# Sliding-window attention and a gated product on one core: the first batch's q and k loaded in blocks, and wide tiles in the second half of the first product

## The chip, the core and the metric

The kernel runs on one core of a Trainium2 chip. A core has five engines with queues of their own: TensorE (PE) for matmuls and transposes, VectorE (DVE), ScalarE (ACT), GpSimd (POOL) and SyncE (SP). ACT, POOL and SP also issue DMAs. The metric is the device time of one execution in microseconds (us); a lower one is better.

## The reference

```python
# q, k, v: (8, 8, 576, 64) float32: batch, head, position, head dimension
scores = matmul(q, k.T) / sqrt(64)
scores = where((rel >= 0) & (rel < 128), scores + slope[head] * -abs(rel), -1e9)   # rel = query - key
attn   = softmax(scores)
x      = matmul(attn, v)                       # -> (4608 tokens, 512)
h      = x @ w_in                              # w_in (512, 2048)
out    = (h * cos(h)) @ w_out                  # w_out (2048, 512); out (4608, 512) float32
```

Each query sees itself and the 127 positions before it, so a block of 128 queries needs its own block of keys and the one before.

## The kernel before

**Work.** All matmuls are bfloat16. The attention is cut into units: for each batch one unit for query block 0 (all heads), two for each of the blocks 1 to 3 (four heads each), and one for the last 64 queries. A unit is: scores on TensorE (L568), in the first units behind a matmul that adds the bias (L582); the exponential on ACT (L595); where there was no bias matmul, a multiplication by the exponential of bias and mask on DVE (L614); the product with v (L630 to L644); its normalisation on DVE (L667 to L681); and a transposition into xT, on TensorE (L702, L721) with a copy, or by a DMA. The 4608 tokens are then worked off in nine chunks of 512. For a chunk the first product (L759, or L784 in chunk 0) makes h in tiles of 128 by 512, ACT the cosine, DVE the product gT, and the second product (L812) the output. While a chunk is in the second product, the next units of attention run.

**Chunk 0** begins when nothing is there yet. Seven units of batch 0 give its 512 tokens. `moe1_block` (L784) works in tiles of 128 tokens by four column blocks, so that it can begin with the first 128 tokens; each tile is 16 matmuls with 128 columns. In the later chunks `moe1` (L759) takes all 512 tokens for one column block, four matmuls with 512 columns.

**The loads.** For the first two batches q and k come in rows: a partition holds several consecutive positions of one head, and TensorE transposes them. `PIECES` (L355) says in which pieces. For batch 0: the first 128 positions in float32 by SP (q) and ACT (k) into `qF`, cast to bfloat16 by DVE or ACT (L378) into `qC` and transposed whole (L504, four transposes of 128 by 128); then positions 128 to 255, 256 to 511 and 512 to 575 by GpSimd, which casts in the DMA (L383), and transposed half by half (L509). Batch 1 comes in one piece for each of q and k. Batches 2 to 7 come in blocks of 128 tokens with all heads side by side (`load_nat`, L402, into `nat`) and are transposed by DMA. v is loaded in such blocks as well (L391), into `vp`. w_in comes in five pieces (L423; the names in the diff count pieces of 256 columns) and w_out in four (L430), all by GpSimd.

**The order.** GpSimd's operations run in the order of the program text. On the other engines a planner (`Plan.schedule`) orders them at build time: every operation has a duration for the engine that is held (`occ`) and one until its result is there (`lat`), due times of loads are estimated from one running clock of the DMA, and at each step the operation that can begin first, by priority `pri`, is taken; for some copies it also chooses between ACT and DVE. While TensorE would stand still near the start, it inserts matmuls on zeros. `emit` then gives each engine its queue in that order, with semaphore waits. A queue is worked off strictly in order: an instruction that waits holds all behind it.

GpSimd's order before is: constants; q and k positions 128 to 255; v block 0; q and k 256 to 511; v block 1; w_in piece 0; v blocks 2, 3; w_in pieces 1, 2-3, 4-5; the ends of q and k; w_in 6-7; batch 1's q and k rows; v block 4; the four quarters of w_out; batch 1's v; batch 2's q and k.

## Time and profile before

| | |
|---|---|
| time, median of 3 runs | 310.25 us (309.75 to 310.46) |
| the profiled execution: time, and span of the core | 310.24 us, 308.4 us |
| busy: TensorE, ScalarE, VectorE, GpSimd | 299.5, 200.3, 195.8, 97.0 us |
| chunk 0's second product (L812) begins | 36.63 us after the span's start |
| moved by GpSimd's DMAs in the whole span | 18.10 MB in 100688 packets |
| moved by the DMAs of SP | 20.33 MB in 49344 packets |

In the rows below, a group of instructions is named by line, engine, operation and tiles (out<-in), with its count; PEld is TensorE's loading of weights, beside the matmuls. A start is in us from the beginning of the span. A DMA's time to landing runs from its issue on the engine to its completion. Where a row covers several issues, their starts follow from the row's length divided by the count.

### The profile page before, as it was taken

Reading aid. Unit: us, or ns where it says so; the run is one execution under the profiler, and the core shown is the slowest. Engines: PE = TensorE matmul, PEld = TensorE weight load, DVE = VectorE, ACT = ScalarE, POOL = GpSimd, SP = SyncE. Lnnn points to the kernel's source line nnn. Section 1 sums busy time; section 2 is a strip of 40 time slices with the busy share of each in tenths; the row PEclk is TensorE's granted clock in tenths of the full one; section 3 lists DMA queues with packets and bytes.
Section 4 is the critical chain, followed back from the end, with each engine's and each line's share of the span. In section 5 each row is a group of like instructions: output and inputs, shape, how many; then the busy total and the mean of one; then the engine's idle time right before and its main releaser. Section 6 shows DMA issues by size and latency. Waiting matters only on the chain.

```text
span 308.4 us, 6675 instructions
## 1 busy us (share of the span) xinstructions
PE 299.5 (97%) x2685; PEld 162.1 (53%) x2726; DVE 195.8 (63%) x409; ACT 200.3 (65%) x267; POOL 97.0 (31%) x122
## 2 busy tenths in 40 slices
PE   8889999999999999999999999999999999999996
PEld 6679755445554455445544554455445554444444
DVE  7688777574668566856785568656966588742000
ACT  6887973875478745873688378746964488752211
POOL 8997200455055505550347123900500000000000
PEclk9999999999999999999999999999999999999999
DMA  9999999999499958998699969995991420001112
GB/s 147 179 204 207 206 162 193 132 183 154 122 121 138 172 98 154 133 175 98 157 114 149 167 88 180 150 184 114 143 113 44 113 70 0 0 0 70 68 71 99
DMA packets 150333, 39.09 MB, mean 127 GB/s; under 512 B 138912, under 2 KB 145312, under 8 KB 150304
## 3 DMA queue, kind: packets, MB, share of 16 engines
q0 software_dynamic: 100688, 18.10, 79.5%
q1 hardware_dynamic: 49344, 20.33, 33.3%
q8 instruction: 21, 0.34, 0.5%
q10 hardware_dynamic: 272, 0.26, 0.3%
q14 instruction: 8, 0.07, 0.1%
HBM read 36.70 MB, written 9.44 MB: 150 GB/s over the span
## 4 chain that ended last, share of the span: by engine, by line
PE 90%; DMA 3%; POOL 2%; ACT 2%; issue 1%; DVE 1%; POOLq 0%; ACTq 0%
PE ps L812 38%; PE ps L759 36%; PE ps L568 5%; PE ps L784 4%; DMA w_inb<-in_moe_w_in_dram 3%; ACT p L595 2%; PE ps L642 2%; PE ps L644 2%; PE ps L630 1%; POOL vp L391 1%; PE ps L509 1%; DVE p L614 1%; PE ps L634 1%; POOL qrows L383 0%; PE ps L721 0%
## 5 line engine op out<-in xcount | busy, mean ns | idle before, releaser
L812 PE MATMUL ps<-w_outb,gT 128*128 128x512 bf16 (+2 forms) x566 | 132.1, 373 | 2.5 <-issue 1.3
L759 PE MATMUL ps<-xT,w_inb 128*128 128x512 bf16 x499 | 113.9, 379 | 0.7
L768 DVE TENSOR_TENSOR gT<-ps,cos 128x512 bf16<-128x512 f32 x128 | 85.1, 688 | 19.6 <-ACT cos L764 14.7
L764 ACT ACTIVATE cos<-ps,halfpi 128x512 f32<-128x512 f32 x128 | 84.6, 687 | 18.0 <-PE ps L759 13.9
L812 PEld LDWEIGHTS ps<-w_outb,gT 128*128 128x128 bf16 x592 | 53.4, 98 | 55.7 <-DVE ob L820 0.3
L595 ACT ACTIVATE p<-ps 128x1024 bf16<-128x1024 f32 x64 | 61.5, 1023 | 31.2 <-PE ps L568 31.0
L759 PEld LDWEIGHTS ps<-xT,w_inb 128*128 128x128 bf16 x512 | 49.0, 98 | 56.2 <-ACT p L595 0.6
L391 POOL DMA_DIRECT2D vp<-in_v_dram x40 | 33.7, 870 | 87.6 <-DMA xT<-xnat 67.4
L614 DVE TENSOR_TENSOR p<-p,emask 128x1024 bf16<-128x1024 bf16 x59 | 39.7, 684 | 27.8 <-ACT p L595 27.8
L819 ACT ACTIVATE ob<-ps 128x512 f32<-128x512 f32 (+2 forms) x21 | 12.1, 576 | 41.6 <-PE ps L812 35.2
L402 POOL DMA_DIRECT2D qnat<-in_q_dram x30 | 25.3, 877 | 22.5 <-DMA qt<-qnat 22.5
L402 POOL DMA_DIRECT2D knat<-in_k_dram x30 | 25.4, 884 | 12.3 <-DMA kt<-knat 9.8
L820 DVE COPY ob<-ps 128x512 f32<-128x512 f32 x16 | 11.0, 685 | 15.8 <-PE ps L812 15.7
L681 DVE TENSOR_TENSOR xnat<-ps,rec 128x256 bf16<-128x256 f32 x48 | 19.9, 421 | 1.3
L568 PE MATMUL ps<-qt,kt 64*128 64x128 bf16 (+1 forms) x576 | 19.4, 211 | 0.3 <-DVE qt L525 0.2
L642 PEld LDWEIGHTS ps<-vp,p 128*128 128x128 bf16 x192 | 14.2, 97 | 9.9 <-issue 6.4
L568 PEld LDWEIGHTS ps<-qt,kt 64*128 64x128 bf16 x576 | 14.5, 94 | 8.7 <-issue 3.5
L642 PE MATMUL ps<-vp,p 128*128 128x65 bf16 x192 | 17.4, 193 | 0.7 <-DVE xT L731 0.5
L644 PE MATMUL ps<-vp,p 128*128 128x65 bf16 x192 | 17.5, 193 | 0.0
L784 PE MATMUL ps<-xT,w_inb 128*128 128x128 bf16 x256 | 16.0, 219 | 0.6 <-DMA w_inb<-in_moe_w_in_dram 0.6
L784 PEld LDWEIGHTS ps<-xT,w_inb 128*128 128x128 bf16 x256 | 14.5, 98 | 1.3 <-DMA w_inb<-in_moe_w_in_dram 0.8
L644 PEld LDWEIGHTS ps<-vp,p 128*128 128x128 bf16 x192 | 13.2, 97 | 2.2
(66 smaller groups left out, 160.9 us busy)
## 6 DMA issues: line engine op xcount, KB each, us to landing
out_dram<-ob SPq DMA_DIRECT2D x35, 256.0 KB, 2.2
vp<-in_v_dram POOLq DMA_DIRECT2D x32, 128.0 KB, 7.1
qnat<-in_q_dram POOLq DMA_DIRECT2D x24, 128.0 KB, 6.5
knat<-in_k_dram POOLq DMA_DIRECT2D x24, 128.0 KB, 5.1
w_outb<-in_moe_w_out_dram POOLq DMA_DIRECT2D x4, 512.0 KB, 21.8
w_inb<-in_moe_w_in_dram POOLq DMA_DIRECT2D x3, 512.0 KB, 12.2
qrows<-in_q_dram POOLq DMA_DIRECT2D x1, 576.0 KB, 15.5
krows<-in_k_dram POOLq DMA_DIRECT2D x1, 576.0 KB, 17.5
```

The costliest lines, as they stand in the source:

```text
L391: op("pool", [lambda e, t=t, rows=rows: e.dma_start(vp[b % 2][0:rows, t, :, 0:64], v[b, :, 128 * t:128 * t + rows, :].rearrange("h p d -> ...
L402: fns.append(lambda e, t=t, rows=rows: e.dma_start(nat[which][0:rows, t, :, :], src[b, :, 128 * t:128 * t + rows, :].rearrange("h p d -> p ...
L568: ins = e.matmul(ps[:, banks[x], c0:c0 + n_], keys_ap(b, x, pr, kc), query_ap(b, x, pr, qb, n_), start=not acc, stop=stop)
L595: op("act", lambda e: e.activation(P[i][:, 0:1024], ps[:, banks[0]:banks[0] + 2, :].rearrange("p a b -> p (a b)"), ACTF.Exp, scale=0.125), ...
L614: op("dve", lambda e: e.tensor_tensor(p, p, m, ALU.mult), r=[("P", i), ("EM", 0), ("EM", 1)], w=[("P", i)], occ=600, lat=690, pri=1)
L642: e.matmul(o, P[i][:, c0:c0 + 128], V[:, qb - 1, h, 0:65], start=True, stop=False)
L644: ins = e.matmul(o, P[i][:, c0 + 128:c0 + 256], V[:, qb, h, 0:65], start=False, stop=True)
L759: op("pe", lambda e, kc=kc: e.matmul(ps[:, bank, :], w_in[:, kc, 128 * fc:128 * fc + 128], xT[:, kc, r0:r0 + CH], start=(kc == 0), stop=(k ...
L764: op("act", lambda e: e.activation(cosb[ci][:, :], ps[:, bank, :], ACTF.Sin, bias=halfpi[:, 0:1]), r=["halfpi"], w=[("B", bank), ("cos", c ...
L768: op("dve", lambda e: e.tensor_tensor(gT[gi][:, fc, :], ps[:, bank, :], cosb[ci][:, :], ALU.mult), r=[("cos", ci)], w=[("B", bank)] + [("g ...
L784: ins = e.matmul(ps[:, bank, 128 * i:128 * i + 128], w_in[:, kc, 128 * fc:128 * fc + 128], xT[:, kc, t0:t0 + 128], start=(kc == 0), stop=( ...
L812: op("pe", lambda e, t=t, fc=fc, bank=bank, j0=j0, j1=j1: e.matmul(ps[:, bank, 0:j1 - j0], gT[gi][:, fc, 128 * t:128 * t + 128], w_out[:, ...
```

## The change

Batch 0's q and k now come in blocks of 128 positions throughout, in two forms, and each is transposed by four whole 128 by 128 transposes. Blocks 0 and 1 come in rows in float32 by SP (k's block 0 by ACT), with a cast each (`load_first`). Blocks 2, 3 and the half block 4 come by GpSimd in the form of `load_nat`, with all heads of a position side by side (`load_block`), into the buffer `nat`, whose lower half of the last block is zeroed first. GpSimd's queue has no load of block 1 any more, and its order is written as a string. Three memsets of v's buffers and others are ordered behind the constants of the mask. In chunk 0 the second half of the first product (column blocks 8 to 15) uses `moe1`, with 512 tokens to a matmul, in place of `moe1_block`; batch 1's row transposes come one tile later among them. The seven first units are planned one at a time. Some of the planner's durations change.

```diff
-        PIECES = {0: [(0, 4, [(0, 4)]), (128, 4, [(0, 4)]), (256, 8, [(0, 4), (4, 8)]),
-                      (512, 2, [(0, 2)])],
-                  1: [(0, 18, [(0, 5), (5, 10), (10, 14), (14, 18)])]}
+        ROWS = [(4, [(0, 4)]), (18, [(0, 5), (5, 10), (10, 14), (14, 18)])]
...
+        def load_first(which, src, n):
+            x = qF[which][n]
+            act = which == "k" and n == 0
+            op("act" if act else "sp", [lambda e: e.dma_start(x[:, :, :], row_ap(src, 0, 128 * n, 4))],
+               w=[("qF", which, n)], dma=f"ld{which}{n}", occ=2000 if act else 700,
+               lat=3300 if act else 4000 if n == 0 else 3950, pri=0)
+            i = x[:, :, :].rearrange("p y (j d) -> p y j d", j=4)
+            o = qC[which][n][:, :, :, :].rearrange("p j y d -> p y j d")
+            op(("act", "dve"),
+               {"act": lambda e: e.activation(o, i, ACTF.Copy),
+                "dve": lambda e: e.tensor_copy(o, i)},
+               r=[("qF", which, n)], w=[("rows", which, 0, n)], occ={"act": 460, "dve": 330},
+               lat={"act": 560, "dve": 410}, pri=2)
...
+        def load_block(which, src, t):
+            rows = 128 if t < 4 else 64
+            op("pool", [lambda e: e.dma_start(
+                nat[which][0:rows, t, :, :],
+                src[0, :, 128 * t:128 * t + rows, :].rearrange("h p d -> p h d"))],
+               r=[("nend", which)] if t == 4 else [], w=[("nb", which, t)], dma=f"lb{which}{t}",
+               occ=900, lat=7 * rows)
...
                 op("dve", lambda e, i=i: e.memset(vp[i][:, :, :, 64:65], 1.0), w=[("vinit", i)],
-                   pri=5 * i)
+                   pri=5 * i, after=[last])
...
+        def block_transposes(names, t, banks):
+            def f(e):
+                ins = None
+                for which, bank in zip(names, banks):
+                    for pr in range(NPAIR):
+                        ins = e.transpose(
+                            ps[:, bank, :].bitcast(BF16)[:, 128 * pr:128 * pr + 128],
+                            nat[which][:, t, 2 * pr:2 * pr + 2, :].rearrange("p h d -> p (h d)"),
+                            ident[:, :])
+                return ins
...
-            sizes = ([[2] * 4] + GROUPS + [[], []])[phase + 1]
+            sizes = ([[1] * 7] + GROUPS + [[], []])[phase + 1]
...
-        load_qk("q", q, 0, 0)
-        load_qk("k", k, 0, 0)
+        for n in range(2):
+            load_first("q", q, n)
+            load_first("k", k, n)
         constants()
-        load_qk("q", q, 0, 1)
...
-        load_qk("k", k, 0, 3)
+        for x in "q2 v0 k2 v1 w0-1 q3 k3 v2 w1-2 v3 w2-4 w4-6 q4 k4 w6-8 qr kr v4".split():
...
         biases()
         for n in range(2):
-            qk_transposes(0, "q", n, [0], OB[0:1])
-            qk_transposes(0, "k", n, [0], OB[1:2])
-        qk_transposes(0, "k", 2, [0], OB)
+            for which, bank in zip("qk", OB):
+                row_transposes(0, which, [bank], n)
+        for t in range(2, 4):
+            for which, bank in zip("qk", OB):
+                block_transposes([which], t, [bank])
...
-        qk_transposes(0, "qk", 3, [0], UB)
-        load_w_in(6, 8)
-        load_qk("q", q, 1)
-        load_qk("k", k, 1)
-        load_v(0, [4])
+        block_transposes("qk", 4, UB)
...
                 for i, (t, f4) in enumerate(order):
-                    moe1_block(t, f4, seq[at % 6])
+                    if i >= 8:
+                        moe1(0, i, seq[at % 6])
+                    else:
+                        moe1_block(t, f4, seq[at % 6])
                     at += 1
-                    if i in (9, 12):
-                        qk_transposes(1, "q" if i == 9 else "k", 0, range(2),
-                                      UB + [seq[at % 6], seq[(at + 1) % 6]])
+                    if i in (10, 13):
+                        row_transposes(1, "q" if i == 10 else "k",
+                                       UB + [seq[at % 6], seq[(at + 1) % 6]])
```

166 lines of the change are left out of this document (77 added, 89 removed).

## The prediction

> **What bounds the kernel now.** I read the page's head first, then the busy time by stage, the waits of the first 37 us, the chain that ended last, and last the DMA issues with their landings.
>
> ```profile
> span 308.4 us, 6675 instructions
> PE 299.5 (97%) x2685; PEld 162.1 (53%) x2726; DVE 195.8 (63%) x409; ACT 200.3 (65%) x267; POOL 97.0 (31%) x122
> ...
> 9.10:17.30 8.20, 7.19 (x138) 5.25 (x140) 5.97 (x18) 6.61 (x9) 8.20 (x13) 1.00 1.68 187
> ...
> 36.60:308.40 271.80, 266.44 (x2101) 134.18 (x2138) 167.91 (x336) 171.45 (x227) 67.16 (x80) 1.00 1.12 119
> ```
>
> The columns of the stages are the stretch, its length, then busy time of PE, PEld, DVE, ACT and POOL, the granted clock, the DMA share and GB/s. TensorE is busy for 299.5 of 308.4 us. From 36.6 us on nothing in the diff changes an instruction's size, and TensorE is busy for 266.44 of 271.80 us there. So the change is worth what it moves the moment at which the second product (L812) of the first chunk can run through, at 36.6 us and just behind. The granted clock is 1.00 in these stages, so no term of the clock enters.
>
> Before that the DMA share is above 1 (1.68): a stream of transfers issued by GpSimd runs without a gap. Where TensorE waits for it:
>
> ```profile
> PE ps L784 <- DMA w_inb<-in_moe_w_in_dram: 0.6, 1, 0.6
> ...
> 8.61 8.67 DMA w_inb<-in_moe_w_in_dram
> ...
> 8.61 2.27 POOL L423 DMA_DIRECT2D w_inb<-in_moe_w_in_dram  x3
> ...
> 12.97 0.70 POOL L383 DMA_DIRECT2D qrows<-in_q_dram  x1
> 13.66 0.71 POOL L383 DMA_DIRECT2D krows<-in_k_dram  x1
> ...
> 15.07 3.00 POOL L430 DMA_DIRECT2D w_outb<-in_moe_w_out_dram  x4
> ...
> w_inb<-in_moe_w_in_dram POOLq DMA_DIRECT2D x1, 512.0 KB, 10.4
> ...
> qrows<-in_q_dram POOLq DMA_DIRECT2D x1, 576.0 KB, 15.5
> ...
> krows<-in_k_dram POOLq DMA_DIRECT2D x1, 576.0 KB, 17.5
> ...
> w_outb<-in_moe_w_out_dram POOLq DMA_DIRECT2D x1, 512.0 KB, 24.6
> ```
>
> The first two lines are the wait (total, times, longest) and the chain's piece (start, length); then come GpSimd's issues (start, length), and single issues with the time to landing. The second weight piece (256 columns) ends the only DMA wait of any size, at 8.61 + 8.67 = 17.3 us. The transfer behind it, columns 512 to 1023, is issued at about 9.4 and lands 10.4 later, at 19.8. Batch 1's q rows land at 12.97 + 15.5 = 28.5, its k rows at 13.66 + 17.5 = 31.2, the last quarter of w_out (issued at about 17.3) at 41.9.
>
> ```profile
> 19.89 0.22 PE ps L784 x4
> ...
> 23.46 0.34 PE ps L509 x8
> 23.81 5.02 PE ps L784 x88
> 28.83 1.13 PE ps L509 x36
> ...
> 36.63 3.18 PE ps L812 x14
> ...
> 40.87 0.75 PE ps L812 x3
> ...
> 54.26 5.83 PE ps L759 x27
> ```
>
> These are pieces of the chain. From 19.89 to 36.63, 16.74 us, it runs on TensorE nearly unbroken. The third quarter of w_out is first used at 40.87; the program has seven matmuls of 216 ns (5.83/27) there before the first that needs the last quarter, so that one starts at about 42.4, half a microsecond after its landing. TensorE's work and the stream thus run neck and neck up to 42 us. A gain needs both to be earlier.
>
> **The change part by part.** *The stream.* SP now brings second q and k blocks in float32, so GpSimd's two 128 KB transfers go. Its two of 256 KB become four 128-token blocks of 128 KB, laid out like a block of v; the two ends of 64 KB become half blocks.
>
> ```profile
> 3.50:4.00 0.50, 0.00 (x0) 0.00 (x0) 0.16 (x1) 1.00 1.09 364
> 5.50:6.50 1.00, 0.00 (x0) 0.00 (x0) 0.00 (x0) 1.00 2.14 158
> 7.00:8.50 1.50, 0.41 (x8) 0.28 (x8) 0.00 (x0) 1.00 1.16 171
> ...
> 2.91 0.94 POOL L391 DMA_DIRECT2D vp<-in_v_dram  x1
> ...
> 4.53 0.71 POOL L383 DMA_DIRECT2D krows<-in_k_dram  x1
> ...
> 6.13 0.76 POOL L423 DMA_DIRECT2D w_inb<-in_moe_w_in_dram  x1
> 6.87 1.78 POOL L391 DMA_DIRECT2D vp<-in_v_dram  x2
> ...
> vp<-in_v_dram POOLq DMA_DIRECT2D x1, 128.0 KB, 4.3
> ...
> krows<-in_k_dram POOLq DMA_DIRECT2D x1, 256.0 KB, 6.4
> ...
> w_inb<-in_moe_w_in_dram POOLq DMA_DIRECT2D x1, 256.0 KB, 7.1
> ...
> vp<-in_v_dram POOLq DMA_DIRECT2D x1, 128.0 KB, 7.2
> ```
>
> The first three lines (busy columns of one tile only; the last number is the GB/s of all DMA) are the float32 loads of SP and ACT (364 GB/s), a block of v (158), and the 256 KB row pieces (171). Removed: 256 KB + 512 KB + 128 KB at 171 GB/s, so 1.53 + 3.07 + 0.77 us. Added: 512 KB + 128 KB in blocks at 158, so 3.32 + 0.83, and 512 KB of float32 at 364, so 1.44. The sum is +0.22 us. By landings it looks better: v's first block lands at 7.2 and the second piece of k at 10.9, so the two row pieces took 3.7 instead of 3.07, while v's third block took 0.9 (14.1, behind the first weight piece at 13.2), four of them 3.4 to 3.6 with the rate's 0.83 or this; that gives -0.1 to -0.3. The rates are means over the DMA engines, the landing is that of the last one. I take the middle of +0.2 and -0.3: the stream from the weights on is 0.05 us earlier, which is nothing.
>
> All this hangs on whether SP's 1.44 us are paid by the same stream. The row at 3.5 us has a DMA share of 1.09 before GpSimd's data flow, and none of the later rows here lies below that, so I see no idle room and take the full 1.44. The other bound is none of it, -1.5 us in all. The Trainium skill, DMA: Bandwidth & Descriptors, section "Issuing engines are not separate DMA queues", says that DMAs of all issuing engines run on the same 16 DMA engines and that issuing from several saves only sequencer time; by it the sum is mine, and without it the stream would be 1.4 us shorter. The trace agrees only as far as that share goes; no run so far shows both kinds side by side.
>
> Within the stream v's last full block moves behind the second weight piece. That piece is earlier by such a block, about 0.9, and its 0.6 us wait goes.
>
> *What is late next.* In the changed program's order TensorE meets the transfer of columns 512 to 1023 earlier: after 32 small matmuls of the first product, it takes 12 that need it, and only then the probabilities-times-v group of the seventh unit. In the kernel before, that group and 16 matmuls of another tile came first. So TensorE stands in order at that landing, 19.8 - 0.05, and behind it are queued that group, the last transposes of x and all the rest. At 19.89 the old kernel had done the same 32 matmuls, and the group too. From there I count differences.
>
> ```profile
> 18.01 0.19 PE L642 MATMUL ps<-vp,p 128*128 128x65 bf16 x1
> ...
> 18.26 0.38 PE L784 MATMUL ps<-xT,w_inb 128*128 128x128 bf16 x4
> ```
>
> The group costs 0.25 (18.01 to 18.26): +0.25. Half of the first product goes from 128 matmuls of 57 ns (5.02/88), 7.30 us, to 32 of 216 ns, 6.91: -0.39. The 8 half-width transposes of the ends (0.34) become 8 whole ones, at 57 ns 0.46: +0.12. The sum is -0.02, so L812 starts at 19.8 + 16.72 = 36.5, 0.1 earlier. The float32 blocks' and the third and fourth blocks' transposes lie before 19.8 and are hidden in that wait.
>
> Batch 1's rows: their transposes now follow the third wide tile. Counting forward from 19.8, with 96 small matmuls (5.5), the group, four transposes of x and eight of the ends (0.7) and three wide tiles of 0.86, TensorE gets there at 28.8, as before (28.83), after the landing at 28.5. The k rows come 36 transposes (1.13) and two wide tiles later, at 31.7 against 31.2. No wait. The last quarter of w_out now has six matmuls ahead of it, so it is wanted 0.1 + 0.2 earlier, at 42.1, with a landing at 41.85: no wait, but only 0.25 us of room. Whatever else TensorE gained, it would lose there.
>
> *The casts and the attention chain.* Two more casts, on ACT and DVE:
>
> ```profile
> 5.00 0.47 DVE L378 CAST qcast<-qfirst 128x512 bf16<-128x512 f32 x1
> ...
> 11.24 0.59 ACT L524 ACTIVATE qt<-ps 128x512 bf16<-128x512 bf16 x1
> ...
> 13.48 3.03 ACT L595 ACTIVATE p<-ps 128x1024 bf16<-128x1024 f32 x3 [0.88 <-PE ps L568]
> 16.74 1.02 ACT L595 ACTIVATE p<-ps 128x1024 bf16<-128x1024 f32 x1 [0.23 <-PE ps L568]
> ...
> L614 DVE TENSOR_TENSOR p<-p,emask 128x1024 bf16<-128x1024 bf16 x59 | 39.7, 684 | 27.8 <-ACT p L595 27.8
> ```
>
> Each is half a microsecond, on engines that wait for loads then. The order also puts the transposes of the third q and k blocks ahead of the second unit's scores, and those of the fourth ahead of the fourth unit's. The fourth k block is the last of the same bytes that in the old stream ended with the first weight piece, at 6.13 + 7.1 = 13.2. Add 0.2 to 0.5 for four transposes and their way to ACT and 0.59 for a copy: the fourth exponential starts at about 14.3 instead of 13.48, and the seventh ends at about 18.6 instead of 17.8. Its group is then ready at 19.3 with the mask (684 ns), while TensorE stands at the weights until 19.8 and works on them until 20.4. So the casts and the late blocks cost nothing, covered by about 1.1 us of that wait; past that cover they cost one to one. GpSimd's second issue (v) waits for a memset that now comes behind the mask's constants, near 3.1; that issue was at 2.91 with a landing 4.3 later, so the queue holds work by then; I put it at nothing, at most 0.2.
>
> The sum: 310.24 us for the profiled execution (median 310.25, so no correction) less 0.1 is **310.1 us**. A change below 0.2%, 0.62 us, is about what a measurement of this kernel cannot tell from none.
>
> **The rivals.** *SP's loads fit beside GpSimd's.* If the float32 rows mostly use gaps of the DMA engines, the stream is up to 1.5 earlier, columns 512 to 1023 land at 18.3 to 18.8, and L812 starts 1.0 to 1.3 earlier; w_out's last quarter at 40.4 keeps pace. The time is 309.0. For it: the rate of GpSimd's own float32-to-bf16 pieces (171 written, 342 read) lies under the 364 of the float32 loads; and a shorter slowest engine works the same way (the landings above). Against it: the share never falls.
>
> *The small packets cost more.* The blocks move 128-byte rows where the pieces moved 512 bytes and more.
>
> ```profile
> vp<-in_v_dram POOLq DMA_DIRECT2D x1, 128.0 KB, 8.6
> ```
>
> v's fourth block, issued at about 7.75, landed at 16.35, 2.25 behind the third, which had taken 0.9. If the six new small-packet transfers meet one such step more, every later landing is 1.4 later, L812 starts at 37.9 and the time is 311.5; it decides from the point where the stream is 0.6 late. The Trainium skill, DMA: Bandwidth & Descriptors, section "Specifications", puts line rate at transfers of 512 B or more, and has a read-modify-write below. By that rule this rival is likelier than the forecast; the trace has 158 against 171 GB/s, a loss of 8%, in the sum already.
>
> *The attention chain decides.* If the fourth blocks land past 14.3 (13.2 and the cover), the seventh unit's group is late behind the weights' 12 matmuls. At 15.2 this gives +0.9: 311.0. For it: six transfers of a new shape lie ahead of them. Against it: the same bytes have landed by 13.2 before.
>
> **How the numbers follow.** The forecast, within 0.6 us of none, 0.42. SP's loads hidden, wholly or enough, 0.36: the sum of landings already leans to that side. Small packets 0.16 and the chain 0.06, together 0.22 slower. The range is 309.0 to 311.2: it holds the faster rival's full price, the chain and the smaller half of the packets' price, and leaves out about 0.15. The forecast alone would be 309.6 to 310.7.
>
> **What would show it.** Right: TensorE waits some 0.5 to 1.3 us for w_inb at 19 to 20 us in front of 12 matmuls; q rows land at 28 to 29, w_out's last quarter near 41.9; L812 starts at 36.3 to 36.8. Wrong: those landings off by a microsecond either way, or a wait of TensorE before 19 us for exponentials that L812's start inherits.

## The result and the profile after

The changed kernel takes 311.58 us (median of 14 runs, 310.85 to 312.87), the kernel before 310.11 us on the same chip (14 runs, 309.49 to 311.73): a ratio of 1.0046, 95% interval 1.0030 to 1.0062. A second set gave 311.81 against 310.02, 1.0060 (1.0042 to 1.0078). So the change costs about 1.4 to 1.8 us, where 310.1 had been forecast and 309.0 to 311.2 allowed.

The page after, and its busy time by stage (the columns as before):

```profile
span 309.2 us, 6447 instructions
...
PE 299.6 (97%) x2569; PEld 158.0 (51%) x2612; DVE 195.5 (63%) x409; ACT 202.5 (66%) x271; POOL 97.6 (32%) x122
```

```profile
9.10:17.30 8.20, 7.12 (x125) 5.10 (x125) 4.86 (x16) 7.03 (x10) 8.20 (x13) 1.00 1.87 180
36.60:308.40 271.80, 266.59 (x2102) 134.19 (x2138) 167.08 (x335) 172.22 (x228) 67.16 (x80) 1.00 1.10 119
```

The totals hardly differ: 0.1 us more work on TensorE, 0.8 us more span (some forty records of matmuls are missing in each). Where they part is read from the moments at which a chunk's first product begins on TensorE. From the timeline of before, chunks 1, 4 and 7:

```profile
54.10 0.59 PE L759 MATMUL ps<-xT,w_inb 128*128 128x512 bf16 x2
...
148.79 0.59 PE L759 MATMUL ps<-xT,w_inb 128*128 128x512 bf16 x2
...
247.51 0.81 PE L759 MATMUL ps<-xT,w_inb 128*128 128x512 bf16 x3
```

and from that of after, where the first row is chunk 0's second product:

```profile
36.30 0.81 PE L838 MATMUL ps<-w_outb,gT 128*128 128x512 bf16 x3
...
53.81 1.03 PE L785 MATMUL ps<-xT,w_inb 128*128 128x512 bf16 x4
...
149.03 0.38 PE L785 MATMUL ps<-xT,w_inb 128*128 128x512 bf16 x1
...
248.34 0.38 PE L785 MATMUL ps<-xT,w_inb 128*128 128x512 bf16 x1
```

Such a moment shows a lead only where the same work lies behind it. How many matmuls of chunk 0's second product are through when chunk 1 begins can be read from TensorE's weight loads of that line (the second count; each matmul has one, and all 592 of this line are there in every profile). In before, in after, and in e2, an experiment told below:

```profile
36.00:54.10 18.10, 13.55 (x55) 5.12 (x59) 1.00 1.99 181
```

```profile
36.00:53.81 17.81, 13.31 (x54) 4.91 (x57) 1.00 1.91 177
```

```profile
36.00:53.66 17.66, 13.80 (x57) 5.01 (x57) 1.00 1.90 182
```

The changed order puts two of these matmuls, 0.43 us at 216 ns each, behind the beginning of chunk 1. At chunk 4 the counts are equal (245), and at chunk 7 too (439).

The weight loads also put right where chunk 0's second product begins in before. Its first two loads, in before and in after, are

```profile
36.39 0.13 PEld L812 LDWEIGHTS ps<-w_outb,gT 128*128 128x128 bf16 x2 [0.25 <-issue]
```

```profile
36.27 0.13 PEld L838 LDWEIGHTS ps<-w_outb,gT 128*128 128x128 bf16 x2 [0.20 <-issue]
```

In after the first matmul follows its load by 0.03, at 36.30. In before the first record of a matmul is at 36.63, behind both loads: it is the second matmul, and the first, at about 36.42, has no record.

| point | before | after | lead (-) or loss | with the same work behind it |
|---|---|---|---|---|
| chunk 0's second product | 36.42 | 36.30 | -0.12 | -0.12 |
| chunk 1 | 54.10 | 53.81 | -0.29 | +0.14 |
| chunk 4 | 148.79 | 149.03 | +0.24 | +0.24 |
| chunk 7 | 247.51 | 248.34 | +0.83 | +0.83 |
| end of the span | 308.4 | 309.2 | +0.8 | |
| time of the execution | 310.24 | 312.10 | +1.86 | |

So in this execution the second product began 0.12 us earlier, as the prediction said, and at chunk 1 that lead was gone. 0.69 us were lost between 54 and 248 us, in code that the diff leaves alone, and 1.06 us outside the span (the time less the span: 1.84 before, 2.90 after). A second profile of the changed kernel has 53.69 for chunk 1, also with 57, which is level with before, a span of 308.8, and 3.01 outside.

The other executions tell of a third thing: the changed kernel's span is 308.7 to 311.1 us, and at or over 309.9 in 5 of its 20 runs; before it was so in 1 of 130 (307.6 to 310.1, median 308.2). The time outside the span is 1.83 to 1.93 us in all 130 runs of before; in the changed kernel 1.8 to 3.0.

The waits of TensorE in the first 37 us of after, and the stream's issues and landings:

```profile
PE ps L516 <- DVE kcast L374: 0.6, 2, 0.3
PE ps L539 <- DVE qt L498: 0.5, 1, 0.5
...
PE ps L521 <- DMA qrows<-in_q_dram: 0.2, 1, 0.2
```

```profile
10.70 0.82 POOL L427 DMA_DIRECT2D w_inb<-in_moe_w_in_dram  x1
```

```profile
w_inb<-in_moe_w_in_dram POOLq DMA_DIRECT2D x1, 512.0 KB, 8.6
...
qrows<-in_q_dram POOLq DMA_DIRECT2D x1, 576.0 KB, 14.3
...
krows<-in_k_dram POOLq DMA_DIRECT2D x1, 576.0 KB, 16.4
...
qfirst<-in_q_dram SPq DMA_DIRECT2D x2, 256.0 KB, 4.8
...
kfirst<-in_k_dram SPq DMA_DIRECT2D x1, 256.0 KB, 5.5
```

Columns 512 to 1023 of w_in land at 10.70 + 8.6 = 19.3. The waits for w_inb are gone; instead TensorE waits for k's cast and for a copy of q, at 7 to 11 us.

### The profile page after: what moved, and what is told of

It is laid out like the page before. It is cut to its first block, busy times and chain, and to the rows that moved or that the text cites. A ratio compares the mean times of both kernels' runs of the same rounds, so it can differ in the third digit from the quotient of the medians.

```text
span 309.2 us, 6447 instructions
## 1 busy us (share of the span) xinstructions
PE 299.6 (97%) x2569; PEld 158.0 (51%) x2612; DVE 195.5 (63%) x409; ACT 202.5 (66%) x271; POOL 97.6 (32%) x122
## 4 chain that ended last, share of the span: by engine, by line
PE 80%; DMA 8%; POOL 5%; ACT 3%; DVE 2%; issue 1%; POOLq 0%; ACTq 0%
PE ps L785 35%; PE ps L838 35%; DMA w_outb<-in_moe_w_out_dram 8%; PE ps L594 5%; ACT p L621 3%; PE ps L668 2%; PE ps L670 1%; POOL vp L394 1%; POOL w_inb L427 1%; PE ps L656 1%; DVE p L640 1%; POOL knat L385 1%; POOL w_outb L434 1%; PE ps L660 1%; POOL qnat L385 1%
## 5 line engine op out<-in xcount | busy, mean ns | idle before, releaser
L785 PE MATMUL ps<-xT,w_inb 128*128 128x512 bf16 x529 | 121.2, 379 | 1.3 <-DVE rec L705 0.5
L794 DVE TENSOR_TENSOR gT<-ps,cos 128x512 bf16<-128x512 f32 x136 | 90.7, 688 | 21.5 <-ACT cos L790 16.6
L790 ACT ACTIVATE cos<-ps,halfpi 128x512 f32<-128x512 f32 x136 | 90.2, 687 | 19.6 <-PE ps L785 15.4
L785 PEld LDWEIGHTS ps<-xT,w_inb 128*128 128x128 bf16 x544 | 51.8, 98 | 59.9 <-ACT p L621 0.6
L845 ACT ACTIVATE ob<-ps 128x512 f32<-128x512 f32 (+2 forms) x23 | 13.3, 578 | 43.7 <-PE ps L838 43.6
L846 DVE COPY ob<-ps 128x512 f32<-128x512 f32 x14 | 9.6, 687 | 16.2 <-PE ps L838 16.1
L705 DVE RECIPROCAL rec<-ps 128x4 f32<-128x4 f32 x48 | 8.2, 176 | 6.2 <-PE ps L670 5.7
## 6 DMA issues: line engine op xcount, KB each, us to landing
qrows<-in_q_dram POOLq DMA_DIRECT2D x1, 576.0 KB, 14.3
krows<-in_k_dram POOLq DMA_DIRECT2D x1, 576.0 KB, 16.4
```

The costliest lines, as they stand in the source:

```text
L785: op("pe", lambda e, kc=kc: e.matmul(ps[:, bank, :], w_in[:, kc, 128 * fc:128 * fc + 128], xT[:, kc, r0:r0 + CH], start=(kc == 0), stop=(k ...
L790: op("act", lambda e: e.activation(cosb[ci][:, :], ps[:, bank, :], ACTF.Sin, bias=halfpi[:, 0:1]), r=["halfpi"], w=[("B", bank), ("cos", c ...
L794: op("dve", lambda e: e.tensor_tensor(gT[gi][:, fc, :], ps[:, bank, :], cosb[ci][:, :], ALU.mult), r=[("cos", ci)], w=[("B", bank)] + [("g ...
```

## The experiments

In most of them "later order as before" means that every operation planned behind chunk 0's first product takes its engine and its place from a table of the plan of before, so that the first phase alone differs (the code in the excerpts of this section is shortened):

```diff
+                mark = len(R.all)          # chunk 0, ahead of load_nat("q", q, 2)
...
+        R.pin_late(mark)                   # engines from the table
         R.schedule(filler=...)
+        R.order_late(mark)                 # places from the table
```

All kernels, each against before on the same chip; "outside" is time less span, "long" the runs with a span of 309.9 us or more, the last column the matmuls and transposes of TensorE's program (two more than the weight loads on the page of each run):

| kernel | median us | ratio (95%) | span, median | long | outside, median (range) | matmuls |
|---|---|---|---|---|---|---|
| before | 310.06 | | 308.2 | 1 of 130 | 1.88 (1.83 to 1.93) | 2728 |
| changed | 311.58 | 1.0046 (1.0030 to 1.0062) | 309.25 | 4 of 14 | 2.0 (1.8 to 2.9) | 2614 |
| e12, changed again | 311.81 | 1.0060 (1.0042 to 1.0078) | 309.2 | 1 of 6 | 2.54 (1.8 to 3.0) | 2614 |
| e1 | 311.38 | 1.0047 (1.0026 to 1.0068) | 308.85 | 3 of 8 | 2.29 (1.8 to 3.0) | 2614 |
| e2 | 310.85 | 1.0018 (1.0006 to 1.0030) | 308.7 | 0 of 12 | 2.18 (2.1 to 2.3) | 2728 |
| e3 | 310.30 | 1.0002 (0.9989 to 1.0014) | 308.4 | 0 of 12 | 1.88 (1.8 to 2.5) | 2632 |
| e4 | 311.29 | 1.0037 (1.0021 to 1.0053) | 309.35 | 3 of 12 | 2.02 (1.9 to 2.2) | 2710 |
| e5 | 310.52 | 1.0013 (0.9999 to 1.0027) | 308.5 | 1 of 12 | 1.93 (1.8 to 2.3) | 2619 |
| e6 | 313.90 | 1.0111 (1.0089 to 1.0133) | 311.8 | 5 of 5 | 2.11 (2.1 to 2.2) | 2724 |
| e7 | 310.77 | 1.0016 (0.9999 to 1.0033) | 308.35 | 0 of 12 | 2.18 (1.9 to 3.7) | 2614 |
| e8 | 311.00 | 1.0027 (1.0013 to 1.0042) | 309.0 | 1 of 12 | 2.05 (1.8 to 2.1) | 2636 |
| e9 | 311.82 | 1.0056 (1.0044 to 1.0068) | 309.7 | 2 of 6 | 2.15 (2.1 to 2.2) | 2770 |
| e10 | 311.14 | 1.0041 (1.0026 to 1.0056) | 308.65 | 1 of 6 | 2.30 (2.0 to 3.3) | 2619 |
| e11 | 310.93 | 1.0037 (1.0024 to 1.0049) | 308.9 | 0 of 9 | 2.12 (2.0 to 3.5) | 2614 |
| e13 | 310.72 | 1.0013 (1.0000 to 1.0025) | 308.45 | 1 of 12 | 1.96 (1.8 to 2.8) | 2742 |
| e14 | 310.81 | 1.0014 (1.0002 to 1.0027) | 308.8 | 0 of 11 | 1.90 (1.8 to 2.1) | 2635 |
| e15 | 311.04 | 1.0027 (1.0016 to 1.0037) | 309.2 | 0 of 11 | 1.82 (1.8 to 1.9) | 2636 |
| e16 | 310.83 | 1.0023 (1.0011 to 1.0036) | 308.4 | 0 of 10 | 2.50 (2.0 to 3.0) | 2614 |
| e17 | 310.73 | 1.0015 (1.0007 to 1.0024) | 308.7 | 0 of 11 | 2.02 (1.8 to 2.2) | 2662 |
| e18 | 311.04 | 1.0035 (1.0024 to 1.0046) | 308.9 | 0 of 11 | 2.14 (2.1 to 2.2) | 2710 |

### Which part of the change: e1 to e4

**e1** is the changed front with the later order as before. 

> The changed kernel, except that every operation created behind chunk 0's first product (second products, later attention, later chunks) stands on the engine and in the order that it has in the kernel before; the first phase is the changed one. Theory 'late order' (the first phase is no slower, the loss comes from the order that the planner made of chunks 1 to 6): ratio 0.998 to 1.001, the wait of L785 for DVE's rec near 185 us is gone. Theory 'front' (loads, casts and tiles of the first phase cost the time wherever it shows): 1.003 to 1.006 as for the changed kernel. Theory 'ends' (the time outside the span grew by about 0.5 to 1.0 us): 1.002 to 1.003 with a span as before.

**e2** is the reverse: the first phase of before, and the later order from the table of the changed kernel. 

> The kernel before with the changed kernel's order and engines behind chunk 0's first product; first phase and loads as before. Theory 'late order': 1.002 to 1.004, with a wait of the first product for DVE's rec in chunk 5. Theory 'front': 0.999 to 1.001. Theory 'ends': 1.000, time less span about 1.9.

**e3** is before with the wide tiles alone, later order as before:

```diff
-                    moe1_block(t, f4, seq[at % 6])
+                    if i >= 8:
+                        moe1(0, i, seq[at % 6])
+                    else:
+                        moe1_block(t, f4, seq[at % 6])
```

> The kernel before with the 512-token tiles for column blocks 8 to 15 alone (row transposes of batch 1 one tile later), late order as before. By the count of the prediction 0.39 us less on TensorE, of which the last quarter of w_out gives back all but about 0.4: ratio 0.998 to 1.000 under 'late order' and 'front' (if the loads cost); 1.003 or more if the wide tiles are the cause.

**e4** is the changed kernel without the wide tiles (the diff above reversed), later order as before. 

> The changed kernel with the 128-token tiles kept in the second half of chunk 0's first product, late order as before. Beside e1 it shows the wide tiles' worth in the new front: 0.000 to 0.0013 above e1. Theory 'late order': 0.999 to 1.002. Theory 'front' with the loads as the cause: 1.004 to 1.007.

Measured: e1 311.38, e2 310.85, e3 310.30, e4 311.29. The wide tiles are worth nothing that shows. The front alone loses about as much as the whole change, and brings the spread; the later order alone loses 0.2%. The intervals are too wide to say whether the two add up. Chunks 1 and 7 of e2 begin at

```profile
53.66 1.03 PE L927 MATMUL ps<-xT,w_inb 128*128 128x512 bf16 x4
...
247.77 0.81 PE L927 MATMUL ps<-xT,w_inb 128*128 128x512 bf16 x3
```

against 54.10 and 247.51 in before. With two matmuls fewer behind it (57), chunk 1 of e2 is level with before; up to chunk 7 the changed later order loses 0.26 us, with the front of before. In e1, which has the counts of before, they begin 0.38 and 0.41 late. The front's 0.4 and the later order's 0.3 come to 0.7 in these profiles, where the first profile of the changed kernel has 0.83. That one has a wait of 0.5 us at 185 us which e2 and the second profile of the changed kernel don't have; which other places of the order cost the rest stays open. A few tenths between single profiles are also within the spread of the executions (before: 307.6 to 310.1).

e4's profiled execution is one of the long ones (span 310.4), and shows what the first two profiles don't (columns: stretch, length, PE busy, granted clock, DMA share, GB/s; then the longest wait):

```profile
7.00:8.00 1.00, 0.40 (x8) 1.00 2.26 179
8.00:9.00 1.00, 0.40 (x4) 1.00 2.37 151
9.00:10.00 1.00, 0.56 (x10) 1.00 1.94 176
10.00:11.00 1.00, 0.47 (x13) 0.84 1.70 185
11.00:12.00 1.00, 1.00 (x8) 0.50 2.32 157
...
13.00:14.00 1.00, 1.00 (x9) 0.50 1.86 183
```

```profile
PE ps L685 <- DVE kcast L543: 1.8, 2, 1.0
```

k's second block was cast from 8.46 on instead of 7.96, TensorE was busy for less than half of 7 to 11 us, and then the granted clock stood at 0.50 for three microseconds. The second product began at 38.22; in the changed kernel's first profile it had begun at 36.30.

### SP's loads, their landing, and the clock: e5 to e9, e11

**e5**: the changed front, with the second blocks from GpSimd in bfloat16.

```diff
-        for n in range(2):
-            load_first("q", q, n)
-            load_first("k", k, n)
+        load_first("q", q, 0)
+        load_first("k", k, 0)
         constants()
+        load_first("q", q, 1)    # rows by GpSimd into a bfloat16 buffer, transposed in halves
+        load_first("k", k, 1)
```

> The changed front, later order as before, but the second blocks of q and k come as bfloat16 rows by GpSimd at the head of its queue, so that SP's second float32 loads and their casts are gone; the third and fourth blocks stay whole blocks. Theory SP: the float32 second blocks, landing at 7.1 and 7.9 us in place of 5.7 and 6.4 and then cast, use up the 1.1 us that the attention chain had; without them the time is that of before, 309.9 to 310.4, and the runs scatter by about 1.5 us like those of before. Theory blocks: the whole blocks on GpSimd's queue and their transposes cost it; 311.1 to 311.5, as with the changed front (311.38). Theory clock: TensorE's idle stretches at 7 to 11 us let its clock drop in some runs; the gaps at 7.5 to 10 us should be gone here, and the longest runs with them: 310.0 to 310.5.

**e6**: the reverse, before with SP's second blocks alone.

```diff
-            if b == 0 and n == 0:
+            if b == 0 and n < 2:         # SP, float32, and a cast
...
-        load_qk("q", q, 0, 1)
-        load_qk("k", k, 0, 1)
-        load_v(0, [0])
         load_qk("q", q, 0, 2)
+        load_v(0, [0])
```

> The front of before with one thing new: the second blocks of q and k come by SP in float32 and are cast, and GpSimd's queue begins with the third; the third to fifth blocks stay rows as before, tiles and later order as before. Theory SP: 310.9 to 311.4, with runs scattered over 2 us or more. Theory blocks: 309.9 to 310.4. Theory clock: between, by how long TensorE idles at 7 to 11 us: 310.4 to 311.2 with some long runs whose mean granted clock is under 1.00.

**e7**: the changed front with one number changed in the plan.

```diff
-               lat=3300 if act else 4000 if n == 0 else 3950, pri=0)
+               lat=3300 if act else 4000 if n == 0 else 5500, pri=0)
```

> The changed front, later order as before, and one planned number changed: the second float32 blocks are planned to land 5.5 us after their issue, as the trace shows them, in place of 3.95 us. That puts 5 more zero matmuls between the first scores and the second transposes, and sorts some of the first 20 us otherwise; no wait on a load goes. Theory SP: the data still come late, 311.0 to 311.5. Theory order: the cost came from an order planned for data that weren't there, 309.9 to 310.5. Theory clock: partly mended, 310.3 to 311.0.

**e8**: the changed front with zero matmuls in two of its waits.

```diff
+                if which == "q" and n == 1:          # behind the transposes of q's second block
+                    for _ in range(12): e.matmul(ps[:, 3, 384:512], zeros, zeros)
...
+                if us[0][0] == (0, 0, 0):            # behind the first unit's product with v
+                    for _ in range(10): e.matmul(ps[:, 5, 0:128], zeros, zeros)
```

> The changed front, later order as before, with 12 zero matmuls (0.67 us at 56 ns) behind the transposes of q's second block and 10 (0.56 us) behind the first unit's product with v, where TensorE waited 0.32 and 0.53 us in the trace of the changed kernel and 1.0 us twice in a longer run. Nothing else moves. Theory clock: TensorE no longer idles at 7 to 11 us, the granted clock stays 1.00 in all runs, the runs above 311.5 are gone, and the median falls to 310.3 to 310.8. Theories SP and blocks: no gain; 311.1 to 311.7, since the zero matmuls can outlast the waits by 0.3 us.

**e9** is e6 with 46 such matmuls behind the transposes of q's first block. 

> The kernel of the sixth experiment (the front of before, second blocks by SP in float32 with casts: 313.9 us, TensorE idle for 3.0 us up to 9.86 us, granted clock 0.50 from 9 to 15 us) with 46 zero matmuls (2.6 us at 56 ns) put on TensorE into that wait; the data come no earlier. Theory clock (the idle stretch itself lowers the clock, and that is most of the 3.6 us): granted clock 1.00 from 9 to 15 us, 311.0 to 312.0. Theory late data (the chain of exps starts 3 us late, the clock adds little): 313.3 to 314.0.

**e11** is e5 with the second blocks left in float32 and cast, but issued by GpSimd. 

> The changed front, later order as before, with the second blocks still float32 and still cast, TensorE's order up to the second scores nearly unchanged, but the loads issued by GpSimd at the head of its queue in place of SP. Theory landing (what costs is that SP's second loads land late and by a different amount from run to run): they land near 5.7 and 6.5, 310.2 to 310.8 with a scatter under 1.2 us. Theory casts (the two casts and the order that the planner makes with them cost it): 311.0 to 311.5.

Measured: e5 310.52, e6 313.90, e7 310.77, e8 311.00, e9 311.82, e11 310.93. SP's loads alone make before slower by 1.1%, more than the whole change does and more than any of the three theories gave; without them the changed front comes to within 0.13%. Theory blocks falls. In e6 GpSimd's queue begins with row pieces of 256 KB, and k's second block lands 6.9 us after its issue (5.5 in the changed kernel, 5.2 in its second profile, 6.0 in e4); TensorE's wait, and the clock by stretches in e6 and then in e9:

```profile
PE ps L674 <- DVE kcast L548: 3.0, 1, 3.0
```

```profile
9.00:10.00 1.00, 0.14 (x2) 0.50 2.02 165
10.00:11.00 1.00, 1.00 (x12) 0.50 1.63 191
...
14.00:15.00 1.00, 1.00 (x26) 0.50 1.38 206
```

```profile
9.00:10.00 1.00, 1.00 (x22) 1.00 1.78 178
```

In e9 the data come 0.2 us earlier (k is cast from 9.13 on) and the clock stays at 1.00. e6 lay 3.65 us behind before (310.25 there), e9 lies 1.80 behind (310.02), by nothing but matmuls on zeros: so some 1.85 us, less what the 0.2 is worth, were the clock, and the rest goes with the late data. In the changed front the clock falls in a few of the runs. Of the 11 long runs of changed, e12, e1 and e4, four have a mean granted clock of 0.994 or 0.995, as 3 us at 0.50 make it; the other seven have 0.999 or 1.000 and were not caught in a profile, so their cause is open. The changed kernel itself has one such run in 20 (e12), and before one in 130, its only long one (0.994). With zero matmuls 1 of 12 (e8) and 0 of 11 (e15) are long. For the median the clock is no explanation: e8 left the span at 309.0, and its 311.00 lies between its two cases.

e7 moved the median: 308.35 for the span against 308.85 in e1, no long run, and chunk 1 at

```profile
53.61 0.59 PE L954 MATMUL ps<-xT,w_inb 128*128 128x512 bf16 x2
```

0.87 us ahead of e1 (both with 59 matmuls behind it), although the loads land as in e1: about 0.5 of the front's cost was an order planned for a landing 1.55 us too early. VectorE's queue shows how. In the changed kernel, as in e1, five memsets stand between the cast of k's second block and the copy of q's, for which TensorE waits 0.5 us; e7 has them ahead of the cast, while the engine waits for the load anyway. The copy in the changed kernel and in e7:

```profile
9.23 0.69 DVE L498 COPY qt<-ps 128x512 bf16<-128x512 bf16 x1
```

```profile
8.48 0.68 DVE L667 COPY qt<-ps 128x512 bf16<-128x512 bf16 x1
```

e11 lies between (310.93; a span of 308.9, no long run): its second blocks land at 5.6 and 6.5, no run is long, and something of the casts and their order stays, so neither of its two theories holds alone.

### The changed kernel itself: e10, e12

**e10** is the changed kernel with the edit of e5 and its own later order. 

> The changed kernel as it is, its own later order too, but the second blocks of q and k by GpSimd as bfloat16 rows at the head of its queue. With the later order of before this front gave 310.52. If SP's float32 loads are what the change loses by and its later order costs 0.3 to 0.5: 310.6 to 311.0. If its later order costs nothing with this front: 310.2 to 310.6. If the rest of the change loses too: 311.2 or more.

**e12** is the changed kernel, unedited. 

> The changed kernel once more, for a second profile of it: its runs spread over 310.85 to 312.87, and the one profile shows a front that is level with before. If the spread comes from SP's second loads, this profile differs from the first in the same measure as its span: k's second block casts later than 7.96 us where the span is over 309.2, and the exps 4 to 6 start later than 14.76 by as much. If the front is the same while the span differs, the spread is made later. Median 311.2 to 311.8.

e10 gave 311.14, between its cases: beside e5 the changed later order costs 0.6 by the medians (0.9 by the ratios), 0.15 of it in the span and most of the rest outside. e12's profile differs little from the first (k cast at 7.67 and not 7.96, the fourth exponential at 14.77 and 14.76), yet its span is 0.4 shorter, of which the first lost 0.3 between 182 and 213 us, where it has the wait of 0.5 us: that part of the spread is made later, and the front's part must be read from long runs such as e4's.

### The time outside the span: e13 to e18

The transfers behind the end of the changed kernel's span (309.2), by queue:

```profile
q8 instruction: 1, 0.02, 2.1%
q14 instruction: 1, 0.01, 0.7%
```

Nothing of the kernel is left there but fetches of instructions; the second profile (3.01 outside) has the same two at 311 us. In the window from 309 to 313 us before has no transfer; its last fetch on q8 comes at about 280 us. In the whole profile of before q8 moved 0.34 MB in 21 packets, so about 16 KB each.

**e13**: before, with 14 zero matmuls behind everything.

```diff
+            if e == "pe":
+                for _ in range(14): h.matmul(ps[:, 5, 0:128], zeros, zeros)   # behind the last product
```

> The kernel before with 14 zero matmuls appended behind TensorE's last product (0.8 us at 56 ns, within the 2.4 us that the last copy and the last store take behind it). Nothing else changes, no instruction moves. Theory program length (TensorE's instructions come in fetches of 16 KB, and the program of the changed kernel, 114 matmuls shorter, ends just behind the start of a further one): these 14 carry the program of before over such an edge too; the span stays at 307.7 to 308.7, the time outside it goes from 1.88 in all runs to 2.0 to 3.0 in some, the median to 310.2 to 310.9, and a fetch of instructions shows at 305 to 312 us. Theory no such thing (the time outside belongs to the second loads or to the later order): 1.88 in all runs, 310.0 to 310.2.

**e14**: e7 with 21 zero matmuls in its waits. 

> The changed front planned for a landing 5.5 us after the issue (310.77, span 308.35 at the median but 1.9 to 3.7 us outside it), later order as before, with 21 zero matmuls more: 9 ahead of the first scores (TensorE waited 0.58 us there), 5 ahead of the transposes of k's second block (0.35), 7 ahead of those of q's third (0.29 after 0.15 of other waiting). Theory program length: the last fetch comes before 303 us, the time outside falls to 2.0 in all runs, 310.0 to 310.5, with a span of 308.0 to 308.4. Theory no such thing: 310.6 to 311.0 as without them. If the zero matmuls outlast the waits by 0.3 us: 0.3 more in either case.

**e15**: the changed kernel with the 22 zero matmuls of e8. 

> The changed kernel, its own later order, with the 22 zero matmuls of the eighth experiment (12 behind the transposes of q's second block, 10 behind the first unit's product with v). Theory program length: the time outside the span falls from 1.8 to 3.0 (median 2.0 and 2.5 in two sets of runs) to 2.0 to 2.1 in all runs; span 309.0 to 309.4; 311.0 to 311.4. Theory no such thing: 311.5 to 312.0, outside again up to 3.0. Theory clock: besides, no run with a mean granted clock of 0.995 or a span over 310.5.

**e16**: the changed kernel with the one number of e7, all orders left to the planner. 

> The changed kernel with one planned number changed and all orders left to the planner: the second float32 blocks land 5.5 us after their issue in place of 3.95. Theory order in the front: with the later order of before this took the span from 308.85 to 308.35; here it should do the same, span 308.6 to 308.9 and 311.0 to 311.3. If the planner's later order then comes out like that of before by chance (it costs 0.7 us from 54 to 248 us in the changed kernel): 310.4 to 310.8. Theory that the data alone count: 311.5 to 311.9.

e13 shows it: 310.72, the time outside up to 2.8, 2.3 or more in 5 of 12 runs where no run of 130 of before had over 1.93. The stores at the end of before (303 to 309 us), and in e13 with a fetch among them:

```profile
out_dram<-ob SPq DMA_DIRECT2D x1, 192.0 KB, 1.9
out_dram<-ob SPq DMA_DIRECT2D x1, 64.0 KB, 1.6
```

```profile
q8 instruction: 1, 0.02, 1.0%
...
out_dram<-ob SPq DMA_DIRECT2D x1, 192.0 KB, 2.8
out_dram<-ob SPq DMA_DIRECT2D x1, 64.0 KB, 2.4
```

In that execution (span 309.9) the fetch falls before the last stores, which land later and lengthen the span too. The profiled execution of e7 shows it as well: its last chunk began 0.4 us ahead of before, a q8 fetch falls among the last stores, and its span is 309.6:

```profile
out_dram<-ob SPq DMA_DIRECT2D x1, 64.0 KB, 3.2
```

That lengthening TensorE's program calls forth a q8 fetch says that q8 carries TensorE's instructions. Counted over all kernels: with 2614 to 2619 matmuls 31 of 77 runs have 2.3 us or more outside, with any other length but e13's 2742 it is 1 of 233. (2742 is 2614 and 128: the lengths that are hit lie one fetch apart if a fetch holds 128 matmuls and their weight loads, which no row shows.) e15 closes the other side: the same changed kernel, 22 matmuls longer, has 1.76 to 1.86 outside in all 11 runs and takes 311.04. e14 has 1.85 to 2.13, but its zero matmuls cost 0.45 of the span, and at 310.81 nothing is won on e7. e16 has the span (308.4) and keeps the edge (2.0 to 3.0); at 310.83 it lies just above its second case, and the one number in the plan has halved the loss of the change. What stays open is why some kernels, e2 with the program length of before among them, lie at 2.1 to 2.2 throughout, where before has 1.88.

**e17** and **e18** are e7 with the last four tiles wide (`i >= 12`) and with none. 

> The changed front planned for a landing 5.5 us after the issue, later order as before, and only the last four tiles of chunk 0's first product 512 tokens wide instead of eight, which makes TensorE's program 48 matmuls longer (2662). Theory order and program length: span 308.3 to 308.6, 1.85 to 2.1 outside in all runs, 310.2 to 310.6, level with before. If the front itself costs more than the planned landing: 310.8 to 311.2.

> The same with no wide tile (2710 matmuls on TensorE): the kernel of the fourth experiment (311.29, spans 308.4 to 310.7) with the one planned landing changed. Theory order: span 308.3 to 308.7 and no run over 309.8; 310.2 to 310.7. Theory that the late data count, whatever the order: 311.0 to 311.4 and spans up to 310.7 as there.

e17: 310.73, a ratio of 1.0015, the time outside 1.84 to 2.15 and no run over 308.9 of span: level with e5, still 0.15% behind before. e18: 311.04, not the 310.2 to 310.7 of theory order: its profiled run had a span of 308.1, but three others 309.5 to 309.7. Against e4 the planned landing took the longest spans away (up to 310.7 there) and 0.45 from the median span, of which 0.25 shows in the time. No version beats before.

## Why the prediction was wrong

**The stream: right.** Forecast for the transfer of columns 512 to 1023 was 19.75, measured 19.3; q's rows 28.5, measured 28.7 (14.39 + 14.3); k's rows 31.2, measured 31.4 (14.99 + 16.4). No landing was a microsecond early, so the rival at 309.0 fell. What the shared transfer cost beyond the forecast was paid by SP's loads themselves, which came later. The Trainium skill, DMA: Bandwidth & Descriptors, section "Issuing engines are not separate DMA queues", says that DMAs started by different engines run on the same 16 DMA engines and interleave. The runs agree: the load of k's second block took 4.9 to 6.2 us beside GpSimd's queue of the changed front (e18, e17), 6.9 beside that of e6, and the same bytes at the head of GpSimd's own queue 4.3 (e11).

The sign that was to go with it is missing. TensorE was to wait 0.5 to 1.3 us for w_inb at 19 to 20 us; in after it comes there a tenth of a microsecond before the landing:

```profile
19.07 0.28 PE L747 MATMUL ps<-ident,xnat 128*128 128x128 bf16 x2
19.31 0.84 PE L810 MATMUL ps<-xT,w_inb 128*128 128x128 bf16 x12
```

The wait that was to cover late data had been used up by then.

**The wide tiles, the group, the ends: right.** -0.02 forecast; e3 measured nothing (1.0002).

**The start of the second product: right in the profiled execution, in part by luck.** It was to begin 0.1 earlier and began 0.12 earlier (36.30; the forecast of 36.5 counts from 36.63, 0.21 too late). But the landing came 0.45 sooner than forecast, and the way from there took 17.0 us, where before has 16.5 from 19.89; 0.2 of the difference is a wait for batch 1's q rows, where the working had none. The last quarter of w_out had 0.25 us of room in the forecast, and the small lead ran into it as said; the chain of after has

```profile
18.57 23.65 DMA w_outb<-in_moe_w_out_dram
...
42.27 1.04 PE ps L838 x4
```

a landing at 42.22, 0.37 later than forecast, with TensorE behind it. That is where the lead ended: the twentieth weight load of the second product is 0.13 us ahead of before, the twenty-fourth 0.18 behind.

**"So the casts and the late blocks cost nothing, covered by about 1.1 us": the first step that failed, as a bound.** The second unit's scores in before and in after, the casts, and the exponentials of after:

```profile
8.45 0.40 PE L568 MATMUL ps<-qt,kt 64*128 64x128 bf16 x8 [0.16 <-DVE qt L525]
```

```profile
10.82 0.40 PE L594 MATMUL ps<-qt,kt 64*128 64x128 bf16 x8
```

```profile
7.96 0.54 DVE L374 CAST kcast<-kfirst 128x512 bf16<-128x512 f32 x1 [0.69 <-DMA kfirst<-in_k_dram]
```

```profile
7.17 0.63 ACT L373 ACTIVATE qcast<-qfirst 128x512 bf16<-128x512 f32 x1 [0.75 <-DMA qfirst<-in_q_dram]
...
14.76 2.97 ACT L621 ACTIVATE p<-ps 128x1024 bf16<-128x1024 f32 x3
...
17.89 1.03 ACT L621 ACTIVATE p<-ps 128x1024 bf16<-128x1024 f32 x1
```

The size of a cast was right, the fourth exponential 0.46 late on the forecast of 14.3, the seventh's end 0.3 (18.92 against 18.6), and in this execution the cover held. But the working costed the casts and the fourth blocks, and never asked when SP's second blocks land. They land at about 7.1 and 7.9, where GpSimd's were at 5.7 and 6.4 (issued at 1.36 and 2.2, 4.3 and 4.2 to landing), and TensorE, in order, stands at them: the second unit's scores start at 10.82 in place of 8.45. In e5, without SP's loads, they start at 8.91, so about 1.9 of the 2.4 us belong to those loads and the order around them, on a chain whose cover was 1.1; in this execution what else came earlier made it good. The order planned for the early landing cost about 0.5 of span (e7 against e1). In e4 a landing half a microsecond later went with a fallen clock and a second product 1.9 us later. Late data alone don't do that: in e17, planned for the later landing, k's second block took 6.2 us and TensorE waited 1.0 us for it, yet the clock stayed at 1.00 and the second product began at 36.18.

**"No term of the clock enters": failed in a part of the runs.** It was read off stages in which TensorE was busy. After the idle stretch that the change made at 7 to 11 us the granted clock dropped to 0.50 for 3 us in e4, and for 6 in e6; e9 puts a price of up to 1.85 us on it there. In the changed kernel itself one run in 20 shows it, so it is a small part of the loss. The Trainium skill, TensorE: Matmul & The Clock Gate, Part 1, says that the clock halves after an idle window of about 3.4 us which runs free of the kernel. The free-running window would explain why only some runs are hit. Against the Trainium skill, e4's TensorE was never idle for more than 1.0 us at a time, and busy for 0.40 to 0.56 of each microsecond; it lost its clock all the same.

**"From 36.6 us on nothing in the diff changes an instruction's size": true, and not enough.** The planner made another order of the same instructions. That lost 0.26 us up to 248 us in e2's profile, whose median span is 0.5 longer than that of before, and 0.69 from 54 to 248 us in the changed kernel's own profile. The prediction had no term for it, on either side.

**"310.24 for the profiled execution (median 310.25, so no correction)": failed.** The 1.84 us outside the span was taken for a constant. It is one of before. The changed kernel has 2.0 and 2.54 at the median of the two sets, up to 3.0. That its program ends just past the start of a 16 KB fetch is what e13, for the program of before, and e15 speak for: e15 takes the time outside back to 1.82 and the whole to 311.04.

So of 1.4 to 1.8 us, 0.2 to 0.7 at the median is the fetch at the end (e15). In e15 0.84 stays (1.0027), the same in e8 with the later order of before; what is left, about 0.3, goes as far as is known with the long runs, which e15 lacks. Of the 0.84, 0.4 goes with the planned landing (e17: 1.0015, without the long runs) or with SP's loads (e5: 1.0013). The last 0.4, in e5 a chunk 1 that begins at 54.38 instead of 54.10, wasn't taken apart.

The rival of dearer packets gave nearly the right time, 311.5, by luck and for a wrong reason: no landing of the stream was 1.4 us late. The chain's rival had the right place, with the second blocks where it named the fourth.

## What to carry to other kernels

When a load moves to another queue, work out its landing first, and follow who stands behind it in the in-order engine; a cover that is used up shows as spread before it shows in a median, so one profile does not see it. If a planner orders the instructions, any edit reorders what it doesn't touch: pin the rest to tell the edit from its shadow, and tell the planner the landings that the trace shows. When you compare moments in two orders, count the work that lies behind each. Time outside the span is a term like any other: compare it across kernels, and look for instruction fetches in the last microseconds.

## What the runs showed of the hardware

- The length of TensorE's program decides on up to 1 us and more at its end: 14 matmuls on zeros behind the last product of before took the time outside the span from 1.83 to 1.93 in 130 runs to 2.3 and more in 5 of 12; 22 more in the changed kernel took it from up to 3.0 to 1.86 at most.
- With a fetch among the last stores these landed 0.8 and 0.9 us later in e13 (2.4 in place of 1.6 us, 2.8 in place of 1.9), and the last one 1.6 us later in e7 (3.2).
- The granted clock can fall to 0.50 without a long wait: four microseconds at a busy share of 0.40 to 0.56, no wait over 1.0 us (e4). With one wait as long and shares of 0.47 to 0.95 it stayed at 1.00 (e17).
- The same float32 load by SP took 4.9 to 6.2 us to land in the profiles of the changed front, and 6.9 beside another queue of GpSimd's (e6).
